# Sliding-window attention and an MLP on one core: another order of the first batch, earlier weight loads, and unused matmuls

## The chip, the cores and the metric

The kernel runs on 1 core of one Trainium2 chip. The metric is the device time of one execution in microseconds (us), and of a kernel the median of its executions. A core has TensorE (matmul; loading weights into its array is a row of its own, PEld), VectorE (DVE), ScalarE (ACT), GpSimd (POOL) and SyncE (SP). Each runs its own instructions in their order and waits on semaphores for the others. Transfers between HBM and the on-chip memory are issued by SP, ACT or POOL, each through its own queue, and are carried out by 16 DMA engines that all queues share.

## The reference

For 8 batches of 8 heads, 576 tokens and 64 numbers a head, the reference computes attention in a window of 32 tokens to either side, and then an MLP on the 4608 tokens:

```python
scores = scale * np.matmul(q, k.transpose(0, 1, 3, 2))
mask = np.abs(pos[:, None] - pos[None, :]) <= 32
scores = np.where(mask, scores, -1e9)
attn = softmax(scores)                       # over the last axis
x = np.matmul(attn, v)  -> [8 * 576, 512]    # heads side by side
h = x @ w_in                                 # 512 -> 2048
out = np.maximum(0.01 * h, h) @ w_out        # 2048 -> 512
```

Inputs and output are float32; the kernel multiplies in bfloat16.

## The kernel before

**Tiles.** Two heads make a pair, so a batch has 4 pairs p, and its 576 tokens make two halves of 288. A *step* i is one pair of one half: i = 8 x batch + 4 x half + p. In PSUM, `score(i)` (L291) writes five matmuls, 544 columns of scores, to the one bank pair `ps`. ScalarE takes the exponent into `e` (L297), and `pr` = `e` x mask is made on POOL, or on VectorE for steps 0 and 1 (L301). `weighted(i)` then runs two matmuls against a block of ones (`s`, L309 and L310: the row sums, already spread over the partitions), five against V (`x`, L317), a reciprocal `r` of `s` on VectorE (L323) and the product `xT` (L325). There is one `s` bank and one `x` bank. `r3` or `xT3` below is that of step 3.

**The MLP.** A *group* g is one half of tokens (288). `h_tile(g, f)`, for f = 0 to 15, multiplies four chunks c of `w_in` with the `xT` of the pairs c = 0 to 3 (L336), and ScalarE writes the leaky ReLU to `gT` (L340). So a group needs the `xT` of its four steps, the last chunk that of the last one. `o_tile(j)` is 16 matmuls of 512 columns against `w_out` (L350), an eviction `o_sb` (L355) and a store (L356). Transposes, h tiles and o tiles take their PSUM from one pool of three buffers, `mmps`.

**Getting a pair ready.** q and k of a pair are loaded as float32 (`qf`, `kf`), cast to bfloat16 (`qb`, `kb`), transposed on TensorE (`tp`) and copied by ScalarE to `qT` and to a block-diagonal `kbd`; v is cast into a block-diagonal `vbd`. `kbd` and `vbd` are first filled with zeros. Below, qb(p,h), kb(p,h), vbd(p,h) and T(p,h) are the casts and transposes of pair p of batch 0; batch 0 is loaded and made ready in two parts, h = 0 and h = 1, by `load_qk0`, `load_v0`, `cast_qk0` (L205: qb on VectorE, kb on POOL), `cast_v0` (L216 on ScalarE, L218 on POOL) and `transposes0` (L229, with L233 and L241 on ScalarE). `t_pair(p, h)` runs both halves of the generator `transposes0(p, h)`: q, then k. Later batches p are written vbd(1,p) for batch 1 in the o tiles, with casts at L187, L195 and L197 and transposes at L258.

**Order.** The kernel is under a manual schedule: each engine does its instructions in the order in which the Python code writes them. For batch 0, that order is written out by hand at the end of the function: steps 0 to 3, then the 16 tiles of h group 0 with steps 4 to 7 and the rest of the transposes between them, then h group 1. `step()` writes score(i+1) and weighted(i). From there on `plan` lists h tiles and quarters of o tiles with an estimated time each, `due` lists transposes and steps with the clock time at which they are to be written, and `spend` writes what is due before each item. During o tiles 0 to 3, batch 1 is transposed (`transposes1`) and its first half attended to (`step1`, steps 8 to 11).

**Queues.** SP issues the loads of q and k, and nearly all of v. The weights are issued by POOL, in four chunks `load_w_in(0..3)` (L411; chunk i serves h tiles 4i to 4i+3) and four `load_w_out(0..3)` (L415; chunk i serves 4 of an o tile's 16 matmuls), and cast to bfloat16 on the way. The first load of batch 1 waits for w_out(1): a copy of 4 bytes from that chunk into the tile `qf0` (L68, the marker) stands ahead of it.

Of the kernel before, what the change touches and what calls it, by code (L numbers as in the profile page):

```python
# [16 lines left out]
def kernel(  # L17
# [182 lines left out]
    def cast_qk0(p, h):  # L200
        for eng, src, dst, part in (
            (nc.vector, qf, qb, PART_Q[h]), (nc.gpsimd, kf, kb, PART_K[h]),
        ):
            c0, c1 = columns(part)
            eng.tensor_copy(  # L205
                out=dst[:, p, c0:c1],
                in_=src[0, p][:, :, c0 * D:c1 * D].rearrange("p a (c d) -> p c a d", d=D),
            )

    def cast_v0(p, h, on_act=False):  # L210
        n0, n1 = PART_V[h]
        for a in range(2):
            r = slice(64 * a, 64 * a + 64)
            to, src = vbd[0][r, p, n0:n1, r], vf[0, p][r, n0:n1]
            if on_act:
                nc.scalar.activation(out=to, in_=src, func=AF.Copy)  # L216
            else:
                nc.gpsimd.tensor_copy(out=to, in_=src)  # L218
# [67 lines left out]
    def score(i):  # L286
        b, hf, p = where(i)
        ps = scps.tile([128, 1024], FP32, name="ps")
        c0 = 512 - HALF
        for blk, q0, n in WIN[hf]:  # L290
            nc.tensor.matmul(  # L291
                ps[:, c0:c0 + n], kbd[b % 2][:, p, blk],
                qT[b][:, p, q0:q0 + n], start=True, stop=True,
            )
            c0 += n
        e = attn.tile([128, NCOL], BF16, name="e")
        nc.scalar.activation(  # L297
            out=e, in_=ps[:, 512 - HALF:512 - HALF + NCOL], func=AF.Exp, scale=scale,
        )
        pr = attn.tile([128, NCOL], BF16, name="pr")  # L300
        (nc.vector if i < 2 else nc.gpsimd).tensor_mul(pr, e, mask[hf])  # L301
        probs[i] = pr
# [41 lines left out]
    def o_tile(j, hook=None):  # L344
# [10 lines left out]
        nc.scalar.activation(out=o_sb, in_=o, func=AF.Copy)  # L355
        nc.scalar.dma_start(out=out[ts(j, 128), :], in_=o_sb)  # L356


    NC = 2 * NPAIR * B
    state = {"tp": 8, "done": 0}  # L360
# [20 lines left out]
    def step():  # L381


        i = state["done"]
        b, r = i // 8, i % 8
        if b > 0:
            upto = 8 * (b + 1) + PLAN[b > 1][0][r]
            step_transposes(max(upto - 1, 8 * (b + 1)))
        if i + 1 < NC and i != 7:
            score(i + 1)  # L390
        weighted(i)
        if b > 0:
            step_transposes(upto)
        if 0 < b < B - 1:
            for p in PLAN[b > 1][1][r]:
                cast_qk(b + 1, p)
                if b + 2 < B:
                    load_qk(b + 2, p)
            for p in PLAN[b > 1][2][r]:
                cast_v(b + 1, p)  # L400
                if b + 2 < B:
                    load_v(b + 2, p)
        state["done"] += 1
# [5 lines left out]
    def load_w_in(i):  # L409
        f = slice(512 * i, 512 * i + 512)  # L410
        nc.gpsimd.dma_start(out=w_in_bf[:, :, f], in_=w_in_r[:, :, f])  # L411
# [7 lines left out]
    def t_pair(p, h):  # L419
        next(t0[p, h])  # L420
        next(t0[p, h])

    cast_qk0(0, 0)
    make_mask(0)
    nc.vector.memset(kbd[0][:, 2:4], 0.0)
    cast_qk0(1, 0)
    for p in range(2):
        nc.vector.memset(vbd[0][:, p], 0.0)
    t_pair(0, 0)
    next(t0[1, 0])  # L430
    score(0)
    next(t0[1, 0])
    cast_v0(0, 0)
    cast_qk0(2, 0)
    for p in range(2, 4):
        nc.vector.memset(vbd[0][:, p], 0.0)
    t_pair(2, 0)
    score(1)
    cast_v0(1, 0, on_act=True)
    cast_qk0(3, 0)  # L440
    load_w_in(0)
    weighted(0)
    t_pair(3, 0)
    score(2)
    cast_v0(2, 0, on_act=True)
    weighted(1)
    load_w_in(1)
    score(3)
    cast_v0(3, 0, on_act=True)
    weighted(2)  # L450
    make_mask(1)
    cast_qk0(0, 1)
    weighted(3)
    state["done"] = NPAIR
    t_pair(0, 1)
    score(4)
    cast_v0(0, 1)
    cast_qk0(1, 1)
    cast_v0(1, 1)


    for f in range(FFC):
        h_tile(0, f)
        if f == 1:
            cast_qk0(2, 1)
            load_w_in(2)
            t_pair(1, 1)
        if f == 3:
            step()
            cast_v0(2, 1)  # L470
            cast_qk0(3, 1)
            load_w_in(3)
            t_pair(2, 1)
        if f == 6:
            step()
            cast_v0(3, 1)
            load_w_out(0)
            t_pair(3, 1)
        if f == 9:
            step()  # L480
            load_w_out(1)
        if f == 12:
            step()
            load_w_out(2)
            load_w_out(3)

    for p in range(NPAIR):
        load_qk(1, p, w_out_bf[0:1, 4, 0:2] if p == 0 else None)
# [39 lines left out]

    def step1():
        i = state["done"]  # L530
        if i == 8:
            cast_v(1, 0)
            score(8)
        if i < 11:
            cast_v(1, i - 7, on_act=i % 2 == 0)
        load_v(2, i - 8)
        step()

    due += [(O_US * (3.9 + 2 * p), transposes1) for p in range(NPAIR)]
    due += [(O_US * (8.9 + 1.6 * p), step1) for p in range(NPAIR)]  # L540
    due.sort(key=lambda t: t[0])
    clock = 0.0

# [40 lines left out]
```

## Time and profile before

| | |
|---|---|
| median of 10 executions | 359.16 us (357.15 to 361.19) |
| the profiled execution | 359.06 us, of which its span is 357.3 |
| TensorE busy | 327.8 us, 92% of the span, 2752 matmuls |
| VectorE, ScalarE, POOL busy | 189.4, 206.5, 175.1 us |
| reciprocals L323 | 64, mean 1957 ns |
| h matmuls L336 and o matmuls L350 on the chain that ended last | 27% and 32% of the span |
| first h tile, first tile of h group 1, first o tile, h group 2 start at | 23.34, 41.89, 49.36, 78.30 us |
| w_in chunks issued at | 10.68, 16.92, 28.09, 32.88 us |
| w_out chunks issued at | 35.68 us, the others from 37.72 |
| first load of batch 1 | 49.77 us |

A line of an answer in order of time has the start in us, the time, engine, line, operation, output and input with partitions x elements and type, and in brackets how long the engine had been idle and what ended that. Where instructions of one kind are merged, "x8" is how many, and the time is from the first's start to the last's end. Matmuls overlap, so a group's time holds a tail behind the last one's issue. A stage's or window's line has the busy time and count of each engine.

### The profile page before, as it was taken

How to read it: one execution, taken by the hardware profiler on the slowest of the kernel's cores; microseconds unless marked ns; L12 is line 12 of the kernel's file. 1: busy time of each engine (PE TensorE's matmuls, PEld its weight loads, DVE VectorE, ACT ScalarE, POOL GpSimd, SP SyncE). 2: the span in 40 equal slices, each digit the busy share in tenths (PEclk: the TensorE clock that was granted, in tenths of full speed). 3: DMA queues.
4: the chain of work that ended last, by engine and by line, in shares of the span. 5: the costliest groups of instructions: out<-in, count | busy, mean ns of one | idle time of the engine just before them, and what ended most of it. 6: DMA issues, size and time to landing. Idle time of an engine off the chain costs nothing.

```text
span 357.3 us, 6972 instructions
## 1 busy us (share of the span) xinstructions
PE 327.8 (92%) x2752; PEld 221.6 (62%) x2752; DVE 189.4 (53%) x208; ACT 206.5 (58%) x447; POOL 175.1 (49%) x215
## 2 busy tenths in 40 slices
PE   2569797789989999999999999999999999999995
PEld 1437654458475676757585676768585666667652
DVE  5875504585545554656654664655564655655200
ACT  4837555459384483838483574838383666646441
POOL 7447934637756454665544553645553554222000
PEclk9999999899999999999999999999999999999999
DMA  7964999967575632534343524443220101010102
GB/s 204 195 117 73 167 208 302 255 188 205 145 185 160 188 74 80 178 102 125 95 131 121 169 68 119 141 140 108 76 62 31 59 2 61 1 61 0 61 10 78
DMA packets 62434, 42.39 MB, mean 119 GB/s; under 512 B 39874, under 2 KB 57794, under 8 KB 62402
## 3 DMA queue, kind: packets, MB, share of 16 engines
q1 hardware_dynamic: 51650, 27.99, 29.7%
q0 software_dynamic: 4224, 4.19, 7.8%
q10 hardware_dynamic: 6528, 9.77, 7.4%
q8 instruction: 21, 0.34, 0.4%
q14 instruction: 11, 0.09, 0.1%
HBM read 36.70 MB, written 9.44 MB: 129 GB/s over the span
## 4 chain that ended last, share of the span: by engine, by line
PE 72%; ACT 7%; DMA 7%; POOL 4%; issue 3%; DVE 3%; ACTq 1%; SPq 0%; POOLq 0%; DVEq 0%
PE mm L350 32%; PE mm L336 27%; PE x L317 3%; PE tp L258 3%; PE ps L291 3%; DMA w_out_bf<-in_moe_w_out_dram 2%; ACT o_sb L355 2%; DVE r L323 2%; PE s L309 2%; DMA vf<-in_v_dram 2%; POOL pr L301 2%; PE s L310 1%; ACT e L297 1%; DMA qf<-in_q_dram 1%; ACT gT L340 1%
## 5 line engine op out<-in xcount | busy, mean ns | idle before, releaser
L323 DVE RECIPROCAL r<-s 128x288 f32<-128x288 f32 x64 | 125.3, 1957 | 93.4 <-PE s L310 93.0
L301 POOL TENSOR_TENSOR pr<-e,mask 128x544 bf16<-128x544 bf16 x62 | 75.2, 1215 | 137.6 <-ACT e L297 135.7
L336 PE MATMUL mm<-xT,w_in_bf 128*128 128x288 bf16 x1024 | 137.2, 289 | 3.3 <-ACT gT L340 1.5
L350 PE MATMUL mm<-w_out_bf,gT 128*128 128x512 bf16 x576 | 132.0, 381 | 0.2 <-ACT o_sb L355 0.2
L336 PEld LDWEIGHTS <-w_in_bf 128*128 128x128 bf16 x1024 | 98.8, 99 | 30.4 <-issue 3.9
L340 ACT ACTIVATE gT<-mm 128x288 bf16<-128x288 f32 x256 | 102.5, 413 | 21.9 <-PE mm L336 8.0
L350 PEld LDWEIGHTS <-gT 128*128 128x128 bf16 x576 | 55.3, 98 | 60.2 <-issue 0.8
L355 ACT ACTIVATE o_sb<-mm 128x512 f32<-128x512 f32 x36 | 21.5, 598 | 85.6 <-PE mm L350 85.6
L297 ACT ACTIVATE e<-ps 128x544 bf16<-128x544 f32 x64 | 39.8, 623 | 19.0 <-PE ps L291 10.2
L275 DVE COPY kbd<-kT 64x576 bf16<-64x576 bf16 x56 | 24.9, 444 | 22.8 <-ACT kT L272 22.4
L197 POOL CAST vbd<-vf 64x576 bf16<-64x576 f32 x52 | 34.5, 663 | 1.7
L325 DVE TENSOR_TENSOR xT<-x,r 128x288 bf16<-128x288 f32 x64 | 29.3, 458 | 7.1 <-PE tp L258 0.5
L291 PE MATMUL ps<-qT,kbd 128*128 128x128 bf16 (+2 forms) x320 | 27.4, 219 | 2.9 <-ACT kbd L241 1.3
L187 POOL CAST kb<-kf 96x768 bf16<-96x768 f32 x28 | 23.1, 826 | 10.5 <-DMA kf<-in_k_dram 10.5
L291 PEld LDWEIGHTS <-kbd 128*128 128x128 bf16 x320 | 21.1, 102 | 11.2 <-ACT kbd L241 2.2
L317 PE MATMUL x<-pr,vbd 128*128 128x128 bf16 (+2 forms) x320 | 26.9, 217 | 0.6 <-DVE xT L325 0.3
L309 PE MATMUL s<-pr,ones_bd 128*128 128x288 bf16 x64 | 19.0, 297 | 6.1 <-DVE r L323 3.2
L317 PEld LDWEIGHTS <-vbd 128*128 128x128 bf16 x320 | 21.6, 101 | 4.9 <-issue 2.3
L266 ACT ACTIVATE qT<-tp 128x576 bf16<-128x576 bf16 x28 | 18.2, 649 | 6.5 <-PE tp L258 5.4
L272 ACT ACTIVATE kT<-tp 128x576 bf16<-128x576 bf16 x28 | 18.2, 650 | 2.6 <-PE x L317 1.4
L187 POOL CAST qb<-qf 96x768 bf16<-96x768 f32 x24 | 19.7, 821 | 0.0
L310 PE MATMUL s<-pr,ones_bd 128*128 128x256 bf16 x64 | 18.2, 284 | 0.0
(43 smaller groups left out, 124.2 us busy)
## 6 DMA issues: line engine op xcount, KB each, us to landing
out_dram<-o_sb ACTq DMA_DIRECT2D x36, 256.0 KB, 2.3
qf<-in_q_dram SPq DMA_DIRECT2D x28, 288.0 KB, 3.2
kf<-in_k_dram SPq DMA_DIRECT2D x28, 288.0 KB, 3.9
vf<-in_v_dram SPq DMA_DIRECT2D x56, 144.0 KB, 3.0
w_in_bf<-in_moe_w_in_dram POOLq DMA_DIRECT2D x4, 512.0 KB, 5.7
w_out_bf<-in_moe_w_out_dram POOLq DMA_DIRECT2D x4, 512.0 KB, 9.2
qf<-in_q_dram SPq DMA_DIRECT2D x8, 144.0 KB, 3.5
kf<-in_k_dram SPq DMA_DIRECT2D x4, 192.0 KB, 3.9
```

The source lines that it names most:

```text
L187: eng.tensor_copy(out=dst[:, p], in_=src[b, p].rearrange("p a (c d) -> p c a d", d=D),)
L197: nc.gpsimd.tensor_copy(out=vbd[b % 2][r, p, :, r], in_=vf[b, p][r])
L291: nc.tensor.matmul(ps[:, c0:c0 + n], kbd[b % 2][:, p, blk], qT[b][:, p, q0:q0 + n], start=True, stop=True,)
L297: nc.scalar.activation(out=e, in_=ps[:, 512 - HALF:512 - HALF + NCOL], func=AF.Exp, scale=scale,)
L301: (nc.vector if i < 2 else nc.gpsimd).tensor_mul(pr, e, mask[hf])
L317: nc.tensor.matmul(x[:, a:a + n], vbd[b % 2][:, p, blk, :], pr[:, c0:c0 + n], start=(n_ == 0), stop=(n_ == len(WIN[hf]) - 1), skip_group_c ...
L323: nc.vector.reciprocal(r, s)
L325: nc.vector.tensor_mul(xT[:, p, t0:t0 + HALF], x, r)
L336: nc.tensor.matmul(h[:, 0:HALF], w_in_bf[:, c, ts(f, 128)], xT[:, c, ds(t0, HALF)], start=(c == 0), stop=(c == DMC - 1),)
L340: nc.scalar.activation(out=gT[:, f, ds(t0, HALF)], in_=h[:, 0:HALF], func=AF.Prelu, alpha=0.01,)
L350: nc.tensor.matmul(o, gT[:, f, ds(128 * j % RING, 128)], w_out_bf[:, f, :], start=(f == 0), stop=(f == FFC - 1),)
L355: nc.scalar.activation(out=o_sb, in_=o, func=AF.Copy)
```

## The change

Batch 0's hand-written order is rewritten, and so are the clock times of batch 1's steps. Nothing else is touched.

- Loads of w_in move up: (0) behind kb(2,0), (1) behind kb(3,0), (2) and (3) behind pr3. w_out(0) stands behind pr4, (1) behind pr5, (2) behind vbd(2,1), (3) behind vbd(3,1).
- vbd(0,0) is cast ahead of the transposes; qb(2,0) is cast ahead of pr0 and qb(3,0) ahead of pr1; the zeros of vbd for pairs 2 and 3 come behind weighted(0) instead of ahead of pr1.
- T(0,1) stands ahead of weighted(3) instead of behind it, and T(1,1) ahead of h group 0 instead of in it. Steps 4 to 7 come behind h tiles 1, 5, 9 and 13 instead of 3, 6, 9 and 12, T(2,1) and T(3,1) behind tiles 4 and 8. qb(2,1) is cast behind xT4, qb(3,1) behind xT5.
- `keep_busy(n)` writes n matmuls of 512 columns, the block of ones against the mask, to a PSUM tile that nothing reads. There are four: 2 ahead of weighted(1), 3 ahead of weighted(2), 3 between T(0,1) and weighted(3), 4 ahead of h group 0.
- In the o tiles, `step1` casts v of the pair of its own step, where before it cast the next pair's; score(8) has an entry of its own; transposes1 come at 3.9 + 1.8p and step1 at 8.6 + 1.7p quarters of an o tile.

```diff
+    def keep_busy(n):
+        t = mmps.tile([128, 512], FP32, name="mm", tag="mm")
+        for _ in range(n):
+            nc.tensor.matmul(t, ones_bd, mask[0][:, 0:512], start=True, stop=True)
...
     for p in range(2):
         nc.vector.memset(vbd[0][:, p], 0.0)
+    cast_v0(0, 0)
     t_pair(0, 0)
     next(t0[1, 0])
+    cast_qk0(2, 0)
+    load_w_in(0)
     score(0)
     next(t0[1, 0])
-    cast_v0(0, 0)
-    cast_qk0(2, 0)
+    cast_qk0(3, 0)
+    t_pair(2, 0)
+    score(1)
+    load_w_in(1)
+    cast_v0(1, 0, on_act=True)
+    weighted(0)
     for p in range(2, 4):
         nc.vector.memset(vbd[0][:, p], 0.0)
-    t_pair(2, 0)
-    score(1)
-    cast_v0(1, 0, on_act=True)
-    cast_qk0(3, 0)
-    load_w_in(0)
-    weighted(0)
     t_pair(3, 0)
     score(2)
     cast_v0(2, 0, on_act=True)
+    keep_busy(2)
     weighted(1)
-    load_w_in(1)
     score(3)
+    load_w_in(2)
+    load_w_in(3)
     cast_v0(3, 0, on_act=True)
+    keep_busy(3)
     weighted(2)
     make_mask(1)
     cast_qk0(0, 1)
+    t_pair(0, 1)
+    keep_busy(3)
     weighted(3)
     state["done"] = NPAIR
-    t_pair(0, 1)
     score(4)
+    load_w_out(0)
+    cast_qk0(1, 1)
     cast_v0(0, 1)
-    cast_qk0(1, 1)
-    cast_v0(1, 1)
+    t_pair(1, 1)
+    keep_busy(4)
     for f in range(FFC):
         h_tile(0, f)
         if f == 1:
+            step()
+            load_w_out(1)
             cast_qk0(2, 1)
-            load_w_in(2)
-            t_pair(1, 1)
-        if f == 3:
+            cast_v0(1, 1)
+        if f == 4:
+            t_pair(2, 1)
+        if f == 5:
             step()
+            cast_qk0(3, 1)
             cast_v0(2, 1)
-            cast_qk0(3, 1)
-            load_w_in(3)
-            t_pair(2, 1)
-        if f == 6:
-            step()
-            cast_v0(3, 1)
-            load_w_out(0)
+            load_w_out(2)
+        if f == 8:
             t_pair(3, 1)
         if f == 9:
             step()
-            load_w_out(1)
-        if f == 12:
+            cast_v0(3, 1)
+            load_w_out(3)
+        if f == 13:
             step()
-            load_w_out(2)
-            load_w_out(3)
...
     def step1():
         i = state["done"]
-        if i == 8:
-            cast_v(1, 0)
-            score(8)
-        if i < 11:
-            cast_v(1, i - 7, on_act=i % 2 == 0)
+        cast_v(1, i - 8, on_act=i % 2 == 0)
         load_v(2, i - 8)
         step()
-    due += [(O_US * (3.9 + 2 * p), transposes1) for p in range(NPAIR)]
-    due += [(O_US * (8.9 + 1.6 * p), step1) for p in range(NPAIR)]
+    due += [(O_US * (3.9 + 1.8 * p), transposes1) for p in range(NPAIR)]
+    due += [(O_US * 6.2, lambda: score(8))]
+    due += [(O_US * (8.6 + 1.7 * p), step1) for p in range(NPAIR)]
```

More of the change, by code (lines that the diff above doesn't have):

```diff
@@ L421, in t_pair @@
         next(t0[p, h])
+    t0 = {(p, h): transposes0(p, h) for p in range(NPAIR) for h in range(2)}
+    def t_pair(p, h):
+        next(t0[p, h])
+        next(t0[p, h])
     cast_qk0(0, 0)
```

## The prediction

> **What bounds the kernel now.** I read the page first, then the engines' busy time by stage, then the chain that ended last, then the first 80 us in order of time. By stage (columns: stretch, its length, then for each engine busy us and count, granted clock, DMA share, GB/s):
>
> ```profile
> 0.00:41.90 41.90, 25.99 (x212) 18.74 (x213) 28.74 (x36) 24.16 (x55) 27.67 (x49) 1.00 0.77 150
> 41.90:49.40 7.50, 7.50 (x62) 5.99 (x62) 0.00 (x0) 6.10 (x15) 6.17 (x7) 1.00 1.15 187
> 49.40:78.30 28.90, 22.90 (x178) 12.79 (x177) 15.61 (x21) 13.50 (x23) 11.83 (x13) 0.94 0.90 243
> 78.30:357.30 279.00, 271.44 (x2307) 184.10 (x2303) 145.05 (x152) 162.78 (x355) 129.42 (x147) 1.00 0.34 99
> ```
>
> From 78.3 us (the first h matmul of group 2) TensorE is busy 271.44 of 279.00 us, in an order that the change leaves alone. So the change is worth what it does to that one time, 78.3 us. Before it lie three stages: batch 0 with the first h group (41.9 us), the second h group (7.5), and four o tiles woven with batch 1 (28.9).
>
> What rules the first stage is seen in VectorE's order of time (start, length):
>
> ```profile
> 18.46 1.96 DVE L323 RECIPROCAL r<-s 128x288 f32<-128x288 f32 x1 [0.17 <-PE s L310]
> 20.52 0.46 DVE L325 TENSOR_TENSOR xT<-x,r 128x288 bf16<-128x288 f32 x1
> 20.90 0.54 DVE L205 CAST qb<-qf 96x384 bf16<-96x384 f32 x1
> 21.36 1.94 DVE L323 RECIPROCAL r<-s 128x288 f32<-128x288 f32 x1
> ...
> 30.14 1.96 DVE L323 RECIPROCAL r<-s 128x288 f32<-128x288 f32 x1 [5.36 <-PE s L310]
> ...
> 33.17 1.96 DVE L323 RECIPROCAL r<-s 128x288 f32<-128x288 f32 x1
> ...
> 35.70 1.96 DVE L323 RECIPROCAL r<-s 128x288 f32<-128x288 f32 x1
> ...
> 39.31 1.96 DVE L323 RECIPROCAL r<-s 128x288 f32<-128x288 f32 x1 [1.09 <-PE s L310]
> ```
>
> These are r2 to r7, the reciprocals of batch 0's steps 2 to 7. Each holds the only s bank, so the next s matmul can't start before it ends. The second h group needs xT7, at 41.84. I follow this chain.
>
> The clock, by windows of 3.4 us (same columns):
>
> ```profile
> 24.90:28.30 3.40, 2.17 (x14) 1.34 (x13) 0.00 (x0) 1.44 (x6) 3.15 (x8) 1.00 0.00 0
> 28.30:31.70 3.40, 3.40 (x27) 2.74 (x26) 1.56 (x1) 2.28 (x6) 1.84 (x3) 1.00 0.58 83
> 62.40:65.80 3.40, 1.39 (x13) 0.74 (x11) 1.03 (x2) 1.79 (x3) 3.25 (x5) 0.95 0.92 209
> 65.80:69.20 3.40, 3.40 (x24) 2.02 (x23) 2.46 (x4) 1.19 (x2) 1.12 (x2) 0.55 1.03 295
> ```
>
> and two h rows in order of time:
>
> ```profile
> 23.34 2.13 PE L336 MATMUL mm<-xT,w_in_bf 128*128 128x288 bf16 x8
> 78.30 3.59 PE L336 MATMUL mm<-xT,w_in_bf 128*128 128x288 bf16 x28
> ```
>
> A 288-column matmul takes 0.24 us in the first row (2.13 less a tail of 0.2, over 8) and 0.123 in the second: half speed up to 31.7 us, although the clock column says 1.00. Full speed comes after the first wholly busy window; a window 64% busy (24.9 to 28.3) had not brought it, and one 41% busy (62.4) was followed by half speed.
>
> **Batch 0 up to r2.** All w_in issues (0.81 to 0.93 us of POOL) move up. w_in(0) comes ahead of kb(3): it ends at 10.0, and kb(3) waited for its data until 10.12 anyway, so 0. qb(2) moves ahead of the first pr, so score 1 can follow kb(2) at 9.6 (10.40 before), and r0 starts at 12.2 (13.13). But the two fills of vbd pairs 2 and 3 (1.15) now stand between xT0 and r1: r1 at 15.9 (15.78), r2 at 18.65 (18.46), xT2 to 21.15, qb(0,1) to 21.75 (21.44). The 2 and 3 fill matmuls ahead of weighted 1 and 2 lie in waits for r0 and r1. Net +0.2, +0.3 at qb.
>
> **Weighted 3 behind T(0,1).** Before, s3 is in front of T(0,1) and starts as r2 ends (20.48). Now T(0,1) and three 512-column fills stand ahead of it, and T(0,1) waits for qb(0,1). T(0,1): 21.8 to 22.3 (0.5, rows at 21.49 to 22.0). A cold 512-column matmul has no row: warm it is 0.217 (16 in 3.47 in the chain), times 0.24/0.123 is 0.42; bounds for three 0.65 and 1.28. I take 1.28, as no wholly busy window ends shortly before. s3 23.6 to 24.25 (0.63). r3 at 24.3 instead of 21.36.
>
> **h group 0 starts behind T(1,1) and four fills.** score 4 24.5 to 25.15, e4 0.62 to 25.8, pr4 1.21 to 27.05, then w_out(0)'s issue 0.8 to 27.9, kb(1,1) 0.40 to 28.3, T(1,1) to 28.6, four fills 1.7 (0.87 warm) to 30.15. Two h tiles at 0.24 x 8 end at 32.1, score 5 0.45, s4 0.63: r4 at 33.2 against 30.14, +3.1. (With the clock open all along: kb 27.1, h 28.2, r4 30.0, -0.1.)
>
> **Steps 5 to 7.** Before, qb(2,1) and qb(3,1) were each cast a step ahead, and r5 and r6 followed at 3.03 and 2.53 us. Now qb(p,1) stands on VectorE right behind the xT of the step, and the next step's score waits for it: from r4, xT ends at 2.5, qb at 3.0, T at 3.35, qT (0.41) and two kbd (0.65) on ScalarE 4.5, score 4.8, s 5.2. So 5.25 a step: r5 38.45, r6 43.7. TensorE's own work in a step, 16 h matmuls 2.0 plus T, score, s and x 1.0, fits inside, and so do POOL's pr 1.21, kb 0.40, vbd 0.86 and issue 0.8 (3.3). r7 needs pr7 (score 7 43.4, e7 44.1, pr7 45.35), r6's end (45.66) and 16 h matmuls (45.95): r7 46.4, xT7 48.9 against 41.84. The 1.26 us wait for w_in(3) in front of s7 is gone, since its issue moves from 32.88 to 19; it is in the difference already. Second h group to 48.9 + 7.5 = 56.4, against 49.36: +7.05.
>
> **Loads.** Before, the DMA engines moved 0 GB/s from 24 to 28 us; w_in(2) and (3) were issued at 28.09 and 32.88, now at 18.2 and 19.0 (behind pr3 on POOL, ahead of the second mask and kb(0,1), which is done at 21.1, before qb(0,1) at 21.75: 0). There they meet the second-half loads on SP's queue, the last of which is issued at 17.87. The four w_out chunks took some 14 us from the first issue at 35.7 to the last landing, so 3.5 a chunk: those loads land at most 7 us later, by 30. Their first user in that stage is T(2,1) at 36.7, so it costs nothing; without that slack it would cost up to 7. w_in(2) is used by f8 after 39. w_out(0), (1), (2), (3) are each issued behind the pr of steps 4 to 7, about 0.8 us ahead of the kb or vbd cast next on POOL; only the first is on the path, and it is counted above. w_out(3) goes out near 46.5 and lands 8 to 12 later (rows 9.2 median, 12.1 longest), by 58.5; the first o tile reaches it at 59.0. The fills' PSUM buffer is one of three; nobody reads it, so it delays no T or h tile.
>
> **Batch 1 and the o tiles.** w_out(1) issued at 34.7 (pr5's end), 5.5 to land as w_in(3) did alone: 40.2; the marker copy 3.85; so batch 1's loads start at 44.0 against 49.77 and end near 58 against 63.7. w_out(2) and (3), two chunks of some 3.5 us of the engines, now fall among them: at worst 65. The first T needs kb(1,0): POOL's eight fills (8.1) end at 55.1, the cast at 56. So the waits on q and k after the first o tile go. What is late next: the casts of v, which before were made a step ahead and now directly ahead of the step that uses them. From o start: o0 3.46; o_sb0 holds T0 (0.85); o_sb1 0.35; x8 waits for vbd(1,0) on ScalarE, behind o_sb1, qT2, kT2, 1.39 (1.8); x9 for vbd(1,1) behind pr9 (0.35); s10 for r9 (1.05), x10 for vbd(1,2) behind o_sb2 (1.1); x11 for vbd(1,3) behind pr11 (0.8). Together 6.3 of waits. Work: 64 o matmuls 13.85, four T pairs 2.05, six scores 1.45, five weighted 2.35, in all 19.7. Bounds of the stage: 19.7 (no wait) and 28.9 (as before). I take 26.0, nearer to the upper row: group 2 starts at 82.45 against 78.30, +4.15.
>
> **Sum.** 359.06 (the profiled execution: span 357.3 and 1.76 around it) + 4.15 = 363.2. The median of the ten runs, 359.16, is 0.1 above that execution. A change within 0.5% (357.36 to 360.96) can't be told from none.
>
> **A rule against the row.** The Trainium skill, "TensorE: Matmul & The Clock Gate", section "Why this matters for your kernels", says that only a TensorE gap of over some 3 us brings the half clock back. Here the longest wait in the window from 62.4 was 2.01 us, and the clock went to 0.55. By the rule the new waits (at most 1.8) leave the clock alone; by the row a stretch with 2.15 of 3.4 us idle may halve it, and the sum would be up to 1.7 more, 364.9.
>
> **Rivals.** *The clock opens early.* From 9.1 to 13.1 TensorE has T, score, s, x and fills nearly without a gap; if that opens the clock and the gaps don't close it, r4 is at 30.0 and the end 3.2 earlier: 360.0, no change. Against it: 19.3 to 21.8 and 25.2 to 27.5 are idle, and windows 41% busy close it. 15%.
> *Faster: the o stage has no waits.* Its place is the x matmuls of steps 8 to 11: if the v casts are done before they come, the stage is 19.7 and group 2 starts at 76.1: 356.9. It decides below 21.9 us (78.3 - 56.4). For it: batch 1 lands 5 us earlier; against it: the casts' places in the queues. 13%.
> *Slower still: the clock closes again* in the thin windows of steps 5 and 6 (2.0 us idle in 3.4) or 10: one or two windows at half speed, 1.7 each: 364.9 to 366.6. 12%.
> The forecast 60%, own range 361.7 to 364.7 (from keep fills at 0.65 instead of 1.28 and hop errors of 0.05 over some 30 hops). That the weights are not earlier at all is excluded by POOL's order. For the range: what is under 358.8 (the faster rival and a little) and over 366.2 makes two in ten. Slower: 60 + 12 less 4 for the forecast's lower tail; same 18, faster 14.
>
> **What would show it.** Right: T(0,1) near 21.8 with r3 near 24.3; first h matmul near 30; r4, r5, r6 5.25 apart; xT7 near 49; x8 to x11 waiting for vbd; group 2 at 82 to 83. Wrong: h matmuls at 0.123 us from the start, r4 near 30, an o stage under 22 us, or batch 1's casts still waiting for DMA after 56.

## The result, and the profile after

The changed kernel takes 361.97 us (median of 15, 360.43 to 364.21) against 359.04 (median of 52, 356.95 to 361.19): 1.0085 times as long, 95% interval 1.0066 to 1.0103. It is slower by 2.9 us. The execution that was profiled took 362.94 us with a span of 361.2, so it lies 1.0 us above its kernel's median; the section after the next comes back to that.

TensorE, VectorE, ScalarE and POOL by stage, in the profile of the changed kernel (stretch, its length, busy us and count of PE, PEld, DVE, ACT and POOL, granted clock, DMA share, GB/s):

```profile
0.00:49.26 49.26, 30.54 (x223) 19.95 (x224) 28.63 (x37) 24.55 (x55) 28.78 (x51) 0.93 0.85 171
...
56.73:82.10 25.37, 20.84 (x179) 11.68 (x177) 13.27 (x18) 13.46 (x23) 10.88 (x12) 1.00 0.79 206
82.10:361.20 279.10, 271.50 (x2307) 184.13 (x2303) 145.36 (x152) 162.65 (x356) 129.42 (x147) 1.00 0.32 96
```

The last stretch is that of before to 0.1 us (279.10, 279.00), so the whole difference, 3.8 us, is made ahead of group 2. There two large amounts stand against each other: batch 0 with the first h group became 7.4 us longer (49.26, from 41.90), and the o tiles with batch 1 3.5 us shorter (25.37, from 28.90).

The first stage by VectorE's rows (in order of time: start, length):

```profile
18.69 1.96 DVE L323 RECIPROCAL r<-s 128x288 f32<-128x288 f32 x1 [0.17 <-PE s L310]
...
21.13 0.54 DVE L205 CAST qb<-qf 96x384 bf16<-96x384 f32 x1
24.07 1.96 DVE L323 RECIPROCAL r<-s 128x288 f32<-128x288 f32 x1 [2.41 <-PE s L310]
...
32.53 1.96 DVE L323 RECIPROCAL r<-s 128x288 f32<-128x288 f32 x1 [5.48 <-PE s L310]
...
37.57 1.96 DVE L323 RECIPROCAL r<-s 128x288 f32<-128x288 f32 x1 [2.06 <-PE s L310]
...
43.03 1.96 DVE L323 RECIPROCAL r<-s 128x288 f32<-128x288 f32 x1 [2.48 <-PE s L310]
...
46.69 1.96 DVE L323 RECIPROCAL r<-s 128x288 f32<-128x288 f32 x1 [1.14 <-PE s L310]
```

These are r2 to r7. r2 is where it was (+0.2), r3 comes 2.7 us later, r4 2.4, and then the steps are 5.04 and 5.46 us apart where they were 3.03 and 2.53. In brackets stands that VectorE now waits for s ahead of every one of them. The same stretch on TensorE:

```profile
21.72 0.42 PE L229 MATMUL tp<-ident,qb 96*128 96x96 bf16 x3 [2.54 <-DVE qb L205]
...
22.10 1.48 PE L363 MATMUL mm<-mask,ones_bd 128*128 128x512 bf16 x3
23.38 0.45 PE L309 MATMUL s<-pr,ones_bd 128*128 128x288 bf16 x1
...
28.24 0.30 PE L229 MATMUL tp<-ident,kb 96*128 96x96 bf16 x2 [0.84 <-POOL kb L205]
28.35 1.91 PE L363 MATMUL mm<-mask,ones_bd 128*128 128x512 bf16 x4
30.05 1.97 PE L336 MATMUL mm<-xT,w_in_bf 128*128 128x288 bf16 x8
...
35.56 0.30 PE L229 MATMUL tp<-ident,qb 96*128 96x96 bf16 x3 [1.36 <-DVE qb L205]
```

T(0,1) waits for qb(0,1), and the three unused matmuls stand between it and s3. Four more stand ahead of the first h tile, at 30.05 instead of 23.34. T(2,1) waits for a cast that comes only behind xT4, and T(3,1), at 40.60, waits as long (1.36 us) for one behind xT5.

In the o tiles, the waits of TensorE in the kernel before, from 49.4 to 78.3 (what waits, for what: us in total, times, longest):

```profile
PE s L309 <- POOL pr L301: 2.9, 2, 2.0
PE ps L291 <- ACT e L297: 1.2, 2, 0.9
PE tp L258 <- POOL kb L187: 0.8, 1, 0.8
...
```

and in the changed kernel, from 56.7 to 82.1:

```profile
PE x L317 <- ACT vbd L195: 2.3, 2, 1.5
PE s L309 <- DVE r L323: 1.0, 1, 1.0
PE x L317 <- POOL vbd L197: 0.7, 1, 0.7
...
```

Before, POOL stood still for loads: its last cast of k, ahead of pr8, waited 1.73 us for its data. In the changed kernel the four casts follow each other:

```profile
61.02 0.83 POOL L187 CAST kb<-kf 96x768 bf16<-96x768 f32 x1 [1.73 <-DMA kf<-in_k_dram]
```

```profile
55.55 3.46 POOL L187 CAST kb<-kf 96x768 bf16<-96x768 f32 x4
```

Now 3.0 us of 4.3 are waits for casts of v, which come late by their place in the order. The loads of batch 1 start here (SP's issues in order of time):

```profile
39.72 0.72 SPq L68 DMA_DIRECT2D qf<-w_out_bf  x1
41.38 0.34 SPq L70 DMA_DIRECT2D qf<-in_q_dram  x1
```

41.38 instead of 49.77: 8.4 us sooner. Of the 3.5 us by which the o stage is shorter, 1.5 are idle time of TensorE (4.53 us, from 6.00). The other 2.1 are busy time (20.84 us, from 22.90) for the same matmuls: in the profile of before, 3.4 us of this stage ran at half clock, behind the wait of 2.0 us for pr8 (the prediction shows this window, from 65.8), and in this profile none did.

### The profile page after: what moved, and what is told of

It is laid out like the page before. It is cut to its first block, busy times and chain, and to the rows that moved or that the text cites. A ratio compares the mean times of both kernels' runs of the same rounds, so it can differ in the third digit from the quotient of the medians.

```text
span 361.2 us, 7003 instructions
## 1 busy us (share of the span) xinstructions
PE 330.3 (91%) x2764; PEld 221.7 (61%) x2764; DVE 191.1 (53%) x208; ACT 206.7 (57%) x447; POOL 176.5 (49%) x215
## 4 chain that ended last, share of the span: by engine, by line
PE 78%; ACT 8%; DVE 5%; issue 4%; POOL 2%; ACTq 1%; DMA 1%; DVEq 0%; POOLq 0%
PE mm L350 34%; PE mm L336 31%; PE x L317 3%; PE ps L291 3%; DVE r L323 3%; PE tp L258 3%; ACT o_sb L355 2%; PE s L309 2%; PE s L310 1%; ACT e L297 1%; ACT kT L272 1%; ACT gT L340 1%; DMA vf<-in_v_dram 1%; ACTq L356 1%; DVE xT L325 1%
## 5 line engine op out<-in xcount | busy, mean ns | idle before, releaser
L340 ACT ACTIVATE gT<-mm 128x288 bf16<-128x288 f32 x256 | 102.4, 413 | 23.6 <-PE mm L336 9.7
L350 PEld LDWEIGHTS <-gT 128*128 128x128 bf16 x576 | 55.1, 98 | 59.9 <-issue 0.6
L275 DVE COPY kbd<-kT 64x576 bf16<-64x576 bf16 x56 | 24.8, 444 | 31.9 <-ACT kT L272 31.5
L187 POOL CAST qb<-qf 96x768 bf16<-96x768 f32 x24 | 19.7, 821 | 0.0
```

The lines of the kernel that those rows point to most:

```text
L187: eng.tensor_copy(out=dst[:, p], in_=src[b, p].rearrange("p a (c d) -> p c a d", d=D),)
L340: nc.scalar.activation(out=gT[:, f, ds(t0, HALF)], in_=h[:, 0:HALF], func=AF.Prelu, alpha=0.01,)
L350: nc.tensor.matmul(o, gT[:, f, ds(128 * j % RING, 128)], w_out_bf[:, f, :], start=(f == 0), stop=(f == FFC - 1),)
```

## The experiments

The theory was the prediction's: the early weights gain in the o stage, while the fills, the casts behind xT, the casts of v and weighted(3) behind T(0,1) cost more than that. The rivals: the clock, and not the order, sets the first stage; and the early weights do nothing, the o stage being shorter for its new clock times. "Group 2" below is the first h matmul of group 2 in each profile (78.30 before, 82.10 in the change). All ratios are to the kernel before, timed beside it, with 95% intervals.

| kernel | median us | ratio | interval | group 2 |
|---|---|---|---|---|
| the change without fills | 359.44 | 1.0016 | 0.9991 to 1.0041 | 79.02 |
| the change, qb and kb a step ahead | 359.43 | 1.001 | 0.999 to 1.003 | 78.64 |
| the change, v a step ahead | 361.1 | 1.0046 | 1.0023 to 1.0069 | 81.36 |
| the change, weighted(3) first | 361.2 | 1.007 | 1.0039 to 1.0101 | 79.19 |
| all four | 355.68 | 0.9899 | 0.986 to 0.9938 | 74.74 |
| before, early weights alone | 354.98 | 0.9882 | 0.9848 to 0.9916 | 74.20 |
| the change, weights late | 368.58 | 1.0267 | 1.0235 to 1.0299 | 86.95 |
| the change again | 363.24 | 1.0104 | 1.0066 to 1.0142 | 83.11 |
| a better order | 352.01 | 0.9796 | 0.9762 to 0.9831 | 71.05 |
| the same again | 351.97 | 0.9809 | 0.9781 to 0.9837 | 70.08 |
| the same with fills in its waits | 351.15 | 0.9788 | 0.9762 to 0.9813 | 71.17 |

"Group 2" is one execution of each kernel, and a stretch of 3.4 us at half clock moves it by up to 1.7 us; the ratios are over all executions. Five of the thirteen profiles have such a stretch in the o stage: before, the change again, without fills, qb and kb ahead, and weights late.

**The change without its unused matmuls.**

```diff
-    keep_busy(2)
     weighted(1)
...
-    keep_busy(3)
     weighted(2)
...
     t_pair(0, 1)
-    keep_busy(3)
     weighted(3)
...
     t_pair(1, 1)
-    keep_busy(4)
```

> The changed kernel without its twelve unused matmuls; all else as it is. My theory: seven of them stand on the path. In the profile after, the three between T(0,1) and weighted 3 hold s3 from 22.1 to 23.4 us (1.3), and the four ahead of h group 0 hold it from 28.35 to 30.05 (1.7, of which a T needs none). Without them r3 starts near 22.8 (24.07), the first h matmul near 27.3 (30.05), r4 near 30 (32.53), and group 2 about 2.5 us earlier: ratio to the kernel before 1.001 to 1.003. Rival: the fills are what opens the clock (it was open by 27 us in the profile after), and without them the stretch to 32 us is all at half speed; then r4 comes less than 1 us earlier or not at all, ratio 1.006 to 1.010.

1.0016 (0.9991 to 1.0041): not to be told from before. VectorE's row of r4 in this kernel:

```profile
30.03 1.96 DVE L323 RECIPROCAL r<-s 128x288 f32<-128x288 f32 x1 [4.51 <-PE s L310]
```

r3 is at 22.55 (24.07 with fills), the first h matmul at 26.97 (30.05), r4 at 30.03 (32.53), group 2 at 79.02 (82.10). The eight h matmuls take 2.12 us against 1.97 with fills, half speed in both. With fills the clock opens soon after, which brings r4 0.6 us nearer, and closes again at 42.0. So the fills put 3.1 us ahead of the first h matmul. That group 2 moves by 3.1 us too is chance: group 1 comes 4.1 us earlier without fills (45.13, from 49.26), as no half clock falls ahead of r7, and the o stage is 1.05 us longer (26.42, from 25.37), as one falls into it. The medians are 2.5 us apart; the ratio falls from 1.0085 to 1.0016, as expected. Steps 4 and 5 stay 5.04 us apart, though here the clock was open from 31.9 on: that has another cause, and it isn't the clock.

**Casts of q and k a step ahead.**

```diff
     cast_qk0(1, 1)
+    cast_qk0(2, 1)
     cast_v0(0, 1)
     t_pair(1, 1)
...
             load_w_out(1)
-            cast_qk0(2, 1)
+            cast_qk0(3, 1)
             cast_v0(1, 1)
...
             step()
-            cast_qk0(3, 1)
             cast_v0(2, 1)
```

> The changed kernel with qb, kb of (2,1) cast ahead of h group 0 and those of (3,1) behind step 4, each a step earlier, as the kernel before had them. My theory: the steps 4, 5, 6, 5.04 and 5.46 us apart, are held by the cast behind xT (TensorE waits 1.36 twice for qb). With the casts ahead, T(2,1) follows f4 at once, r5 comes 3.7 behind r4, r6 4.0 behind r5, r7 2.5 behind r6; xT7 near 45.2 instead of 49.2, and group 2 near 78 instead of 82.1: ratio 0.997 to 0.999. Rival: the distance of the steps is set by something else (pr on POOL, score and s behind kbd, the h matmuls), then r5 and r6 move by less than 0.5 each and the ratio stays at 1.006 or more.

```profile
35.60 1.96 DVE L323 RECIPROCAL r<-s 128x288 f32<-128x288 f32 x1 [0.70 <-PE s L310]
...
39.61 1.96 DVE L323 RECIPROCAL r<-s 128x288 f32<-128x288 f32 x1 [1.49 <-PE s L310]
```

These are r5 and r6 in VectorE's order of time; r4 is at 31.93 and r7 at 42.07. The distances are 3.67, 4.01 and 2.46 us, where the change has 5.04, 5.46 and 3.66. Group 1 starts at 44.64 instead of 49.26. Of these 4.6 us, 2.8 lie between r4 and r6, where the casts stand, and 1.2 between r6 and r7, where the change ran at half clock. Only 3.5 us are left at group 2 (78.64): its o stage takes 26.5 us instead of 25.4, with the waits for v still in it and a stretch at half clock (eight o matmuls at 71.75 took 3.37 us, where those of the change at 76.40 took 1.89). The ratio is 1.001 (0.999 to 1.003), above the expected 0.997 to 0.999.

**Casts of v a step ahead in the o tiles.**

```diff
         i = state["done"]
-        cast_v(1, i - 8, on_act=i % 2 == 0)
+        if i < 11:
+            cast_v(1, i - 7, on_act=i % 2 == 0)
...
-    due += [(O_US * 6.2, lambda: score(8))]
+    due += [(O_US * 6.2, lambda: (cast_v(1, 0), score(8)))]
```

> The changed kernel with batch 1's v casts a step ahead, as the kernel before had them (vbd(1,0) on POOL with score 8, then on ScalarE, POOL, ScalarE). My theory: x8, x10 and x11 wait 1.53, 0.82 and 0.66 us for their vbd in the profile after; these waits go, some of it into the wait of the next s for r, so group 2 starts 1.5 to 3 us earlier: ratio 1.000 to 1.004. Rival: the reciprocals, one s bank, set the pace of the o stage (r8 68.68, r9 72.91, r10 75.37, r11 78.80), or v's loads come later than the earlier casts: then under 0.7 us, ratio 1.006 to 1.010.

The waits of TensorE in its o stage:

```profile
PE s L309 <- DVE r L323: 1.3, 1, 1.3
PE s L309 <- POOL pr L301: 0.7, 1, 0.7
...
```

Waits for vbd are gone and others stand there: with 0.5 for xT and 0.3 for o_sb, 2.8 us in place of 4.3. The stage is 23.85 us instead of 25.37. This execution's first stage happened to be 0.8 us longer (group 1 at 50.04), so group 2 moved only to 81.36; the ratio is 1.0046 (1.0023 to 1.0069), a little above the expected 1.000 to 1.004.

**Weighted(3) ahead of T(0,1).**

```diff
     cast_qk0(0, 1)
+    weighted(3)
     t_pair(0, 1)
     keep_busy(3)
-    weighted(3)
```

> The changed kernel with weighted 3 ahead of T(0,1) and the three fills, where the kernel before has it. My theory: s3 then follows the end of r2 (20.65 in the profile after) instead of the fills (23.38); r3 starts near 21.7 (24.07). But score 4 still stands behind T(0,1) and the fills, so it ends about 1 us earlier only (24.0), and with it pr4, kb(1,1), the first h matmul (29.0) and r4 (31.5): ratio 1.004 to 1.007, that is 0.6 to 1.6 us less than the change. Rival: r3 and xT3 are what h group 0 waits for, and the 2.4 us go through in full: ratio 1.001 to 1.003.

r3 comes at 21.30, 2.8 us sooner, but T(1,1) still waits for kb(1,1), until 27.01: kb(1,1) stands on POOL behind pr4 and pr4 behind score(4), which T(0,1) and the fills hold up as before. The first h matmul is at 28.85 and r4 at 31.26, 1.3 us sooner than in the change. The ratio, 1.007 (1.0039 to 1.0101), can't be told from the change's own. This profile is also one in which the clock behaved differently (below), so not all of the 1.3 us need be the edit's, nor of the 2.9 us by which group 2 is sooner: the execution, 360.02 us, was 1.2 us quicker than its kernel's median.

**All four together.** The four diffs above in one kernel.

> The changed kernel with four things taken back at once: no fills, weighted 3 ahead of T(0,1), the casts of (2,1) and (3,1) a step earlier, v's casts of batch 1 a step earlier. What is left of the change is the early weights, the order of the first casts and fills with zeros, T(1,1) ahead of h group 0 and the later steps. Theory: the four costs add up (2.5 + 1.0 + 3.5 + 2.0 = 9.0) until batch 1's data is the bound; group 2 near 73 to 75 instead of 82.1: ratio 0.983 to 0.990. Rival: they overlap, for instance because the same wait for kb(1,1) stands behind fills and weighted 3; then 4 to 6 us come back, ratio 0.992 to 0.998.

0.9899 (0.986 to 0.9938), group 2 at 74.74: 7.4 us gained. Between the profiles the four alone add up to more, 10.2 us; by the ratios they add up to 0.0198 against 0.0186, which is no difference given the intervals. One overlap is seen in the profiles: the wait of T(1,1) for kb(1,1) (2.04 us, till 26.86) comes up as soon as the fills are gone, so the first h matmul is at 27.00 here and at 26.97 without fills alone. What is left of the change is faster than before by one per cent. That is the early weights, the order of the first casts, T(1,1) ahead of h group 0 and the new clock times; the next kernel has the early weights alone.

**Only the early weights, in the kernel before.**

```diff
     cast_qk0(2, 0)
+    load_w_in(0)
...
-    load_w_in(0)
+    load_w_in(1)
     weighted(0)
...
     weighted(1)
-    load_w_in(1)
     score(3)
+    load_w_in(2)
+    load_w_in(3)
...
     score(4)
+    load_w_out(0)
...
-            load_w_in(2)
...
             step()
+            load_w_out(1)
...
-            load_w_in(3)
...
-            load_w_out(0)
+            load_w_out(2)
...
-            load_w_out(1)
+            load_w_out(3)
...
-            load_w_out(2)
-            load_w_out(3)
```

> The kernel before with nothing but the eight weight loads issued behind the POOL work behind which the change has them (w_in behind kb(2,0), kb(3,0) and two behind pr3; w_out behind pr4, pr5, vbd(2,1), vbd(3,1)). My theory: this part of the change is the gain that the rest gives away. The wait for w_in(3) ahead of s7 (1.26) goes, w_out(0) ahead of kb(1,1) costs 0.8, and batch 1's loads start near 41 instead of 49.8, so that the o stage loses its waits on q, k and v: 28.9 us become 22 to 24. Group 2 near 72 to 74 instead of 78.3: ratio 0.983 to 0.988. Rival: earlier loads only trade one wait for another (the casts, pr on POOL, the eight fills of kbd and vbd on POOL), ratio 0.996 to 1.002.

0.9882 (0.9848 to 0.9916), at the upper edge of what was expected, and as fast as the kernel with all four taken back: what that one keeps beside the early weights is worth nothing that can be seen. Its o stage, by windows:

```profile
49.30:74.20 24.90, 21.11 (x179) 12.13 (x177) 15.01 (x20) 13.41 (x23) 11.89 (x13) 1.00 0.94 241
```

The first q of batch 1 is cast at 48.30 (52.99 before), and the stage takes 24.90 us with the old clock times and the old casts of v. The first stage still ends at 41.81. So the loads alone took 4.0 us from the stage, and the new clock times gave none of it: 2.2 us are idle time (3.79, from 6.00), and 1.8 busy time, as no half clock falls into this stage. The gain is not only the clock's: the 12 executions of before with a mean clock of 1.000, in which it stayed open once it had opened, have a median of 358.16 us, and this kernel is 3.2 us below even these. On the way the wait for w_in(3) (1.26 us) went, and that for kb(1,1) grew from 1.23 to 2.05 us, because w_out(0)'s issue now stands ahead of it on POOL, besides vbd(0,1).

**The change with its weights late**, at the places of before; vbd(2,1) is ahead of kb(3,1) again, as it was there.

```diff
     cast_qk0(2, 0)
-    load_w_in(0)
...
     score(1)
-    load_w_in(1)
     cast_v0(1, 0, on_act=True)
+    load_w_in(0)
     weighted(0)
...
     weighted(1)
+    load_w_in(1)
     score(3)
-    load_w_in(2)
-    load_w_in(3)
...
     score(4)
-    load_w_out(0)
...
             step()
-            load_w_out(1)
             cast_qk0(2, 1)
+            load_w_in(2)
...
             step()
-            cast_qk0(3, 1)
             cast_v0(2, 1)
-            load_w_out(2)
+            cast_qk0(3, 1)
+            load_w_in(3)
...
-            load_w_out(3)
+            load_w_out(0)
         if f == 13:
             step()
+            load_w_out(1)
+            load_w_out(2)
+            load_w_out(3)
```

> The changed kernel with its weight loads issued late again, where the kernel before has them among POOL's work (w_in 0 behind kb(3,0), 1 behind pr2, 2 and 3 behind kb(2,1) and kb(3,1), all of w_out behind vbd(3,1)). Theory: the early weights hide how much the rest of the change costs. w_out then goes out near 45 us, its chunks land 3.5 us apart to 60, batch 1's loads start near 58 instead of 41, and the o stage waits for q, k and v: group 2 at 88 to 92 instead of 82 to 83, ratio 1.025 to 1.035. Rival: the changed kernel's steps are so late that batch 1 is not what it waits for; then the ratio is 1.010 to 1.018.

1.0267 (1.0235 to 1.0299), as expected, with group 2 at 86.95, sooner than the expected 88 to 92. TensorE's and SP's rows of this kernel:

```profile
44.33 1.16 PE L336 MATMUL mm<-xT,w_in_bf 128*128 128x288 bf16 x8 [2.18 <-DMA w_in_bf<-in_moe_w_in_dram]
...
68.58 0.41 PE L291 MATMUL ps<-qT,kbd 128*128 128x96 bf16 x5 [2.87 <-DVE kbd L275]
```

```profile
57.08 0.34 SPq L70 DMA_DIRECT2D qf<-in_q_dram  x1
```

Waits for w_in are back (another, of 1.20 us, is at 38.31), batch 1's loads start at 57.08, and the scores of batch 1 wait for up to 2.87 us. So the early weights are worth 1.2% in the old order and 1.8 points in the new one (1.0267 to 1.0085).

**The change, unaltered, a second time.**

> The changed kernel as it is, to see how its executions differ: they lay between 360.4 and 364.2 us, and the profiled one, 362.9, in the upper half. Theory: the place of the clock's windows of 3.4 us is free against the kernel's start, and decides whether the fills and the first h tiles run at half or full speed; a second profile with other windows shows another start of the first h matmul (28.5 to 30.3) and of r4 (30.5 to 33.3) and the same 3.7, 5.04 and 5.0 us between the later steps; ratio 1.007 to 1.010. Rival: the spread comes from the transfers; then r4 is at 32.5 again and the o stage differs.

1.0104 (1.0066 to 1.0142). Its profiled execution, 363.86 us, has group 2 at 83.11. Up to the start of group 1 (49.10) it agrees with the first profile to 0.4 us; after that it differs at one place (windows, and one of TensorE's rows):

```profile
72.60:76.00 3.40, 1.55 (x13) 0.67 (x11) 3.27 (x4) 2.02 (x4) 1.22 (x1) 1.00 0.92 216
76.00:79.40 3.40, 3.40 (x13) 1.47 (x14) 1.62 (x2) 0.56 (x1) 2.48 (x3) 0.52 0.42 100
```

```profile
76.30 3.50 PE L350 MATMUL mm<-w_out_bf,gT 128*128 128x512 bf16 x8
```

In the first profile the same eight o matmuls took 1.89 us, at 76.40, behind the same wait. The clock had closed in the one execution and not in the other, though TensorE had been busy nearly alike in the 3.4 us before: 1.57 us here, 1.61 there. The theory expected another start of the first h tiles, and that didn't come (29.71, with r4 at 32.36). The difference is in the o stage, as the rival had it, but it is the clock's and not the transfers'.

**A better order.** Early weights in the order of before, and on POOL what TensorE waits for next put first: kb of pairs 1 and 2 and vbd of pairs 0 and 1 ahead of the first w_out issue and of pr4. With kb of pair 2 its qb moves up on VectorE, w_out(1) is issued behind pr4, and batch 1 has the clock times of the change, with v a step ahead. Against the kernel with the early weights alone:

```diff
     t_pair(0, 1)
-    score(4)
-    load_w_out(0)
-    cast_v0(0, 1)
     cast_qk0(1, 1)
+    cast_v0(0, 1)
+    cast_qk0(2, 1)
     cast_v0(1, 1)
+    load_w_out(0)
+    score(4)
+    load_w_out(1)
...
         if f == 1:
-            cast_qk0(2, 1)
             t_pair(1, 1)
...
             step()
-            load_w_out(1)
...
-        if i == 8:
-            cast_v(1, 0)
-            score(8)
...
-    due += [(O_US * (3.9 + 2 * p), transposes1) for p in range(NPAIR)]
-    due += [(O_US * (8.9 + 1.6 * p), step1) for p in range(NPAIR)]
+    due += [(O_US * (3.9 + 1.8 * p), transposes1) for p in range(NPAIR)]
+    due += [(O_US * 6.2, lambda: (cast_v(1, 0), score(8)))]
+    due += [(O_US * (8.6 + 1.7 * p), step1) for p in range(NPAIR)]
```

> The kernel before with the early weights, and two things that the profiles asked for: kb and vbd of (1,1) and kb of (2,1), vbd(0,1) are cast on POOL ahead of pr4, in its idle 20 to 24 us, so that T(1,1) doesn't wait for kb(1,1) (27.67 in the kernel with the early weights alone); and batch 1's clock times as in the change, with score 8 and the first v cast on their own ahead of step 8. Theory: r4 3 us earlier (near 28), xT7 near 39 instead of 41.8, the o stage 23.9 as with the v casts ahead; group 2 near 70.5 instead of 74.2: ratio 0.975 to 0.981. Rival: with TensorE earlier, batch 1's loads are the bound (the DMA engines need some 55 us for batch 0, the weights and batch 1); then group 2 stays at 72.5 or later, ratio 0.983 to 0.988.

r4 is at 28.05 (30.88 with the early weights alone), group 1 at 38.62 (41.81), group 2 at 71.05 (74.20), and the o stage is as long (24.96, 24.92; 23.9 was expected), so the gain is made ahead of r4. The transposes of kb(1,1) come at 25.94 instead of 27.67; and the clock opens at 26.1 instead of 32.3, so the eight h matmuls behind them take 1.14 us instead of 2.12. 352.01 us, 0.9796 of before (0.9762 to 0.9831), beats both kernels. Run again:

> The faster kernel of the last comparison (the kernel before with early weights, four POOL casts ahead of pr4, batch 1's new clock times) once more, as the measure for the next kernel on the same chip. Expected: ratio 0.976 to 0.983, group 2 near 71.

351.97 us, 0.9809 (0.9781 to 0.9837).

**Fills where TensorE truly waits.** The better order with 1, 2 and 3 unused matmuls ahead of weighted 1, 2 and 3, in the waits for r.

```diff
+    keep_busy(1)
     weighted(1)
...
+    keep_busy(2)
     weighted(2)
...
+    keep_busy(3)
     weighted(3)
```

> The same kernel with unused matmuls only where TensorE waits for a reciprocal and nothing else stands behind them: 1 ahead of weighted 1 (wait 0.67 us), 2 ahead of weighted 2 (1.04), 3 ahead of weighted 3 (1.52), at 0.43 us each at half speed. Theory: fills are worth something only if the clock opens before the first h tiles at 23.8 us and stays open; then those tiles take 0.123 instead of 0.24 us a matmul, and r4 comes up to 1.3 us earlier: ratio up to 0.004 below the kernel without them. Rival: the windows fall as they like, the clock opens in some executions and closes again in the waits (at full speed a fill lasts only 0.22), and the kernel is within 0.002 of the one without fills, or slower if a fill holds an s matmul back.

0.9788 (0.9762 to 0.9813), against 0.9809 (0.9781 to 0.9837) without: no difference. By windows:

```profile
20.00:23.40 3.40, 2.05 (x21) 1.23 (x21) 3.19 (x5) 1.06 (x4) 2.84 (x9) 0.97 1.22 237
23.40:26.80 3.40, 3.18 (x18) 1.92 (x17) 1.33 (x3) 2.15 (x6) 3.27 (x5) 0.53 1.20 223
```

The fills do what they are for: TensorE is busy for 3.22 of the 3.40 us from 16.6, and s3 then takes 0.30 us at 20.43, full speed. But the first window shown is 2.05 us busy, and the clock is closed again in the second. What was won was given back within 7 us.

## Why the prediction was right, and where its sizes were off

**Sign and mechanism held, but for a part of the o stage.** The forecast was 363.2 us with group 2 at 82.45; the profiled execution took 362.94 with group 2 at 82.10. The forecast moved one profiled execution, 359.06, by 4.15; measured were 3.9 between the two profiled executions and 2.9 between the medians.

| step of the sum | forecast | measured |
|---|---|---|
| r1, r2 | 15.9, 18.65 | 16.07, 18.69 |
| T(0,1), s3, r3 | 21.8, 23.6, 24.3 | 21.72, 23.38, 24.07 |
| kb(1,1) cast, first h matmul | 27.9, 30.15 | 27.78, 30.05 |
| r4, r5, r6, r7 | 33.2, 38.45, 43.7, 46.4 | 32.53, 37.57, 43.03, 46.69 |
| last wait for xT7 ends | 48.9 | 49.26 |
| first load of batch 1 | 44.0 | 41.38 |
| o stage: waits | 6.3 | 4.3 by the view of waits |
| o stage: length | 26.0 | 25.37 |

**Weighted(3) and the fills.** Right in place and size: T(0,1) waits for qb(0,1), three cold matmuls (1.28) hold s3, four more hold the first h tile at 30. That they are on the path was shown by leaving them out: the first h matmul comes 3.1 us sooner, and the median is 2.5 us less.

**Half speed up to r4: mis-sized.** The prediction took TensorE at half speed up to r4, since no wholly busy window ended shortly before. But 3.04 us of 3.40 were enough. The clock of the changed kernel, by windows that lie within 0.5 us of its changes (in the trace it opens at 24.91, is at half from 28.32 to 31.73 and again from 41.97 to 45.39):

```profile
21.90:25.30 3.40, 3.04 (x20) 1.80 (x18) 1.23 (x1) 1.21 (x4) 0.00 (x0) 1.00 1.20 221
25.30:28.70 3.40, 0.76 (x6) 0.41 (x7) 1.65 (x3) 0.89 (x3) 2.83 (x5) 0.94 0.89 145
28.70:32.10 3.40, 3.40 (x18) 1.86 (x17) 0.00 (x0) 0.99 (x4) 0.29 (x1) 0.55 0.91 147
...
38.60:42.00 3.40, 1.67 (x17) 0.95 (x15) 1.84 (x3) 1.96 (x7) 2.62 (x5) 1.00 0.15 25
42.00:45.40 3.40, 3.40 (x21) 2.45 (x22) 2.27 (x2) 1.37 (x3) 1.93 (x4) 0.50 1.08 166
```

It opened after the first of these, was of no use in the second, in which TensorE waited, and closed again for the third, in which the four fills and the first h tiles stand. It was open again by s4, which took 0.29 us at 32.10; so r4 came 0.7 us earlier than forecast.

**A step of 5.25 us: right.** 5.04 and 5.46 (43.03 less 37.57), with both waits for qb in the trace; without fills, where no half clock touches these steps, both are 5.04 to 0.01. The experiment with the casts a step ahead shows the cause: 3.67 and 4.01. From r6 to r7 the forecast had 2.7 and the trace 3.66. The window from 42.0 ran at half speed, so the 16 h matmuls ahead of s7 took 3.18 us instead of the forecast's 2.0. This is the rival "the clock closes again", at one of the places it named, and at 1.2 us instead of 1.7; only some of it shows at the end, because r4 to r6 were early. That xT7 came within 0.4 us of the forecast is thus partly luck: the clock made r4 0.7 us early and the step to r7 1.0 us long.

**The rule against the row.** The Trainium skill, "TensorE: Matmul & The Clock Gate", section "Why this matters for your kernels", would have the clock stay open with no gap over some 3 us. The row of before spoke against that, and so do these: the longest wait in the window 38.6 to 42.0 was 1.36 us, and the half clock followed. In the better order with fills no wait in the window ahead of the half clock was over 0.41 us. The measurements decide: waits far below 3 us brought the half clock here. The longest wait doesn't tell when: 0.41 us in one window was followed by it, and 1.53 us in a window of the change (65.9 to 69.3) was not. The busy share of the window tells it at both ends, and not between (the counts stand in the last section).

**Loads and o stage: direction right, three terms off.** The early w_in loads did meet batch 0's second half on the DMA engines, and as forecast that cost nothing: T(2,1) and T(3,1) waited for casts, and these for no load. The marker copy was taken at 3.85 us from its row of before; 1.66 were measured (39.72 to 41.38), so batch 1's loads began 2.6 us sooner than forecast. It did not help, since POOL's eight fills of the block-diagonal tiles hold its first cast until 55.55, as forecast (55.1). Of the waits, x8, s10, x10 and x11 came as forecast (1.5, 1.0, 0.8 and 0.7 us against 1.8, 1.05, 1.1 and 0.8); T0 and x9 did not wait. By TensorE's idle time, 4.53 us, that is 1.8 less; but it was busy for 20.84 us where the forecast's work was 19.7, so the stage is only 0.6 us shorter than forecast. Casting v a step ahead took away 1.5 us of it, and the faster rival (no waits, 19.7 us) was out of reach for every kernel here: the shortest o stage is 23.85, since waits for r and pr come up behind those for vbd.

**The gain of the o stage: right in size, in part by luck.** The forecast took all of before's 28.9 us but 19.7 for waits, and put 6.3 us of waits in their place. But TensorE idled for only 6.00 us in that stage of before, less than those 6.3; its other 22.90 us were busy, with 3.4 of them at half clock. So by its own terms the forecast gained nothing on waits. Its 2.9 us came from work counted at full speed against a row that holds a half clock, and that the half clock would not come back is no term of the sum. In the first profile of the change it didn't (3.5 us gained), in the second it did, and there the stage takes 26.54 us.

**The median is 1 us below the profiled execution.** The times of one kernel go with the clock that the execution was granted. Each of the 22 executions of the change has a mean granted clock on record:

| mean clock | executions | us |
|---|---|---|
| 0.985, 0.990 | 5 | 360.43 to 360.85 |
| 0.981, 0.995, 1.000 | 4 | 361.28 to 361.97 |
| 0.976 | 3 | 362.55 to 362.77 |
| 0.991 | 5 | 362.65 to 363.92 |
| 0.986 | 5 | 362.58 to 364.21 |

Both profiled executions are of the last two groups (0.991 and 0.986). The kernel before has such groups too: of 57 executions with a clock on record, the 12 at 1.000 took 356.8 to 358.6 us, and the 7 at 0.988 to 0.991 took 360.0 to 361.2. The clock isn't all of a spread: the better order run again took 351.03 to 353.29 us at 0.998 to 1.000. So the 1 us between profile and median goes with the clock pattern that the profile happened to catch, and with it most of the 1.2 us by which the forecast is above the median. What the pattern of the change's quickest group is, no trace here shows. The prediction's rival "the clock opens early" (360.0 us) is a candidate: the profile with weighted(3) first, at 360.02 us and clock 0.990, had its clock open early. Three fills took 0.81 us at 15.40 (the same three 1.48 at 15.85 in the change), TensorE was busy for 0.81 us of the window from 16.6, and the half clock came back (the window behind it):

```profile
20.00:23.40 3.40, 2.99 (x19) 1.76 (x20) 3.19 (x5) 0.94 (x3) 1.00 (x3) 0.52 1.23 241
```

That is argued from a neighbour, and stays open for the change itself.

## What to carry to other kernels

- A gain in one stage and a loss in another can be one edit: with earlier weights the o stage took 3.5 to 4 us less (some half of it less waiting, the rest a half clock that did not come), and the order written around them gave away more. Taking each part of such an edit alone, in both directions, told them apart here in seven kernels.
- Before putting unused work or a "just in time" cast into a gap, see what is behind it in its own engine's order. A cast behind the result of the step is on the path of the next step (5.0 us a step against 3.7), and a fill costs what it lasts when the gap ends before it does.
- The one thing to give priority to was the queue that serves several stages: on POOL, the casts TensorE waits for next ahead of issues and products that nothing waits for yet was worth 3 us on top of the early weights (354.98 to 352.01). Some 1 us of it is the clock, which opens sooner; a cast on VectorE and batch 1's clock times moved in the same kernel and were not tried apart.

## What the runs showed of the hardware

- In all 13 profiles the clock changes at moments that lie whole multiples of 3.41 us apart. By the windows between these moments, up to 345 us: the clock opened after each of the 30 windows at half clock in which TensorE was busy 85% or more, and after none of the 80 at 83% or less.
- The half clock came back after all 13 windows at full clock that were busy 46% or less, and after none of the 1168 busier than 60%. Between 47% and 60% it came after four (49%, 50%, 50% and 60%) of 22. The longest wait in a window was 0.41 us in one that was followed by the half clock, and 1.53 us in one that was not.
- Half speed doesn't come at the same place in every execution: in the change it came at 42.0 in both profiles, and at 76.1 in one only, behind a window busy 46% in that one and 47% in the other. The early weights alone had a mean clock of 0.998 to 1.000 in all four executions, which spread by 0.07 us; the change, at 0.976 to 1.000, spread by 3.8 us (360.4 to 364.2). The better order spread by 1.4 and 2.3 us at 0.998 to 1.000, and what causes that wasn't tried.
- The clock column says 1.00 ahead of its first change although the matmuls run at half speed (288 columns in 0.24 us, later 0.123), so the mean clock of an execution doesn't count the time before the first opening: by it alone a lower clock need not be a longer time, as the table shows.
- POOL's fills of 128x1152 in the changed kernel took 1.05 us each, but 1.46 for the three that began at 49.21, 50.62 and 53.03. What makes them longer wasn't tried.
